# Unread products in the waits of a start-up, and another order of its first five chunks

## The chip, the cores and the metric

One core of a Trainium2 chip runs the program; the others are idle. The metric is the time of one execution on the device, in microseconds, as the median of several runs. Engines are named as in the profile: PE multiplies matrices (PEld is its weight load), DVE, ACT and POOL work element by element, SP issues most of the transfers (DMA). Each engine takes its own instructions in the order in which the program wrote them.

## The reference

Three stages follow each other. A recurrence per head with a 40x40 state, over 768 steps of 4x8 heads:

```
y[t]  = r[t] . state
Sa    = state . a[t]
state = state * w[t] - Sa (x) b[t] + v[t] (x) k[t]
```

Its output, 3072 tokens of 320 numbers, goes through a dense layer pair, `max(0.01 h, h)` of `h = x @ w_in` (320x2048), then `@ w_out` (2048x320), and then through a layer of eight experts, of which each token takes the one with the largest gate (320x1024, relu, 1024x320, times the gate's probability).

## The kernel before

The recurrence is cut into 24 chunks of 32 steps, all 32 heads together. A chunk `c` has a part that needs no state, and one that does.

The part without state (`prep`, lines 199 to 283): load `in`, the decays and `a` (`load1`), and `KB`, the keys and `b` (`load1b`); clamp and check the decays (steps a), scan them on DVE (b), scale the queries on POOL and take reciprocals (c), scan backwards on DVE (d), scale the keys on POOL and DVE (e), keep the queries in DRAM (f). Then four products with their evictions by DVE and ACT (G, H, I, J are the products on line 259, g, h, i, j the evictions on lines 264 and 265, into `Ms` and `KBr`), and z, which writes the small triangular matrices `Ms` to `Pq` by four transfers (line 277) and copies `Ms` and `KBr` to DRAM (line 280). Chunk 0 works in `KB`, `AtI`, `Ms`, `KBr`; chunks 1 and 2 keep the same things in pieces of the tiles `woh` and `wol`, which are free as yet; from chunk 3 on it is chunk 0's tiles again.

From `Pq` of several chunks a table T of inverses is made (`halves`): one transpose on DVE into `Tinv` (line 332), 28 small products and sums (lines 342 and 348), one transpose into `TT` (line 356). For chunks 0 and 1 (the word A in the order) this runs on DVE, for chunks 2 and 3 (B) on POOL.

The part with state: `l2`, `l3` load what the chunk needs; `s1` multiplies the state into the chunk (line 388), `s2` makes three products, with T, with `NT`, with T again (line 403), each after an eviction of the one before; `s3` makes the next state (428), `s3x`, `s4`, `s5` make the output (446, 458, 475), `s6` turns the state round (493). Then `s1` of the next chunk.

The dense layers work on pairs of chunks in half steps, the word H: eight products for 128 of the 2048 columns (`layer1`, line 705, into the banks psH), activation on ACT, DVE and POOL, six products of the second layer (line 721). Their weights come in 102 pieces of 256 columns, the word +: a load issued by ACT (line 610), a guard on ACT, three operations on DVE (lines 575, 577, 579), a cast on ACT and a difference on DVE (line 639 or 647).

What comes in which order is written out by hand: the string `START` for chunks 0 to 4, then `STEP`, `LATE`, `END` for one chunk each. `play` reads the words one after another and writes the instructions of each; p is one step of a later chunk's `prep`, u and v are one step of an inverse. So the order of words is the order on every engine. `START` ends in the profile near 218 us. The word F calls `keep_warm`, and no string before the change holds it.

Of the kernel before, what the change touches and what calls it, by code (L numbers as in the profile page):

```python
# [11 lines left out]
F32 = mybir.dt.float32  # L12
# [10 lines left out]
C = 32  # L23
# [13 lines left out]
LOAD, SPLIT = 18, 27  # L37

START = (
# [9 lines left out]
)  # L49
STEP = (  # L50
    "w s6a.-1 s1 s6b.-1 H H H s2 H H p w p p s3a H l2.1 H p w p w p w p w p s3b p s3x H H s4a p p s4b H p H w s5a s5b H p H p H w H w p H l3.1 "
# [449 lines left out]
class Moe1:  # L501


    def __init__(s, tc, ctx, i, k, xT, x2d, tbl, psH):
        s.tc = tc
        nc = s.nc = tc.nc
        s.i, s.k, s.xT, s.x2d, s.tbl, s.psH = i, k, xT, x2d, tbl, psH
        s.bank = lambda: s.psH.tile([128, 512], F32, name="psH")
        s.wide = mybir.dt.size(i["hwi"].dtype) == 8
        pool = lambda x, n, b: x.enter_context(tc.tile_pool(name=n, bufs=b, side="right"))  # L510
        s.r1, s.r2 = pool(ctx, "mr1", 1), pool(ctx, "mr2", 2)
        inner = s.inner = ctx.enter_context(ExitStack())
        s.psX = inner.enter_context(tc.tile_pool(name="psX", bufs=1, space=PSUM, side="right"))
        c = s.p1 = pool(inner, "mp1", 1)
        s.p2, s.p3 = pool(inner, "mp2", 2), pool(inner, "mp3", 3)
        s.wih = c.tile([128, 2, FF], F32R, name="wih")
        s.wil = c.tile([128, 2, FF], F32R, name="wil")
        s.wis = c.tile([128, FF], F32R, name="wis")

        s.tri = s.r1.tile([128, 128], BF16, name="tri")  # L520
        nc.gpsimd.memset(s.tri, 1.0)
        nc.gpsimd.affine_select(out=s.tri, in_=s.tri, compare_op=ALU.is_ge, fill=0.0, base=-1, pattern=[[1, 128]], channel_multiplier=-1)
        s.ones = s.r1.tile([128, 128], BF16, name="ones")
        nc.gpsimd.memset(s.ones, 1.0)
        s.raws = s.r1.tile([128, 4, 2 * DM], I32, name="raws")
        s.wg = s.raws.bitcast(F32).rearrange("p a (b d) -> p (a b) d", b=2)
        s.junk = s.r1.tile([128, DM], BF16, name="junk")
        s.run = s.r1.tile([128, E], BF16, name="run")
        s.code = s.r1.tile([128, E], F32, name="code")
        nc.gpsimd.iota(s.code, pattern=[[-1, E]], base=E, channel_multiplier=0, allow_small_or_imprecise_dtypes=True)  # L530
        s.ecap = s.r1.tile([128, E], F32, name="ecap")
        nc.gpsimd.iota(s.ecap, pattern=[[CAP, E]], base=0, channel_multiplier=0, allow_small_or_imprecise_dtypes=True)
        s.ids = s.r1.tile([128, NC], I32, name="ids")
        for b in range(B):
            for t in range(2):
                nc.gpsimd.iota(s.ids[32 * b:32 * b + 32, t::2], pattern=[[2 * C, NC // 2]], base=S * b + (C - BIG) * t, channel_multiplier=1)
        s.x2c = x2d.rearrange("(b c t) d -> c b t d", b=B, t=C)
        s.least = s.r1.tile([128, 1], F32, name="least")
        nc.gpsimd.memset(s.least, 2.0 ** -30)
        s.fill = s.r1.tile([128, 32], I32, name="fill")  # L540
        nc.gpsimd.memset(s.fill, BIG)
        s.none = s.r1.tile([128, 32], I32, name="none")
        nc.gpsimd.memset(s.none, 0)

    def lend(s):

# [146 lines left out]
    def layer1(s, f):  # L693
# [1 line left out]
        if f == 0:  # L695
            s.xh, s.xl = s.next
        o = slice(128 * f, 128 * f + 128)
        ps = s.psH.tile([128, 512], F32, name="psH")
        terms = [
            (s.wih[:, 0, o], s.xh[:, 0]), (s.wih[:, 1, o], s.xh[:, 1]), (s.wis[:, o], s.xh[:, 2]),  # L700
            (s.wih[:, 0, o], s.xl[:, 0]), (s.wih[:, 1, o], s.xl[:, 1]), (s.wil[:, 0, o], s.xh[:, 0]), (s.wil[:, 1, o], s.xh[:, 1]),
# [116 lines left out]
def stepwise(tc, ctx, i, k, x2d, tbl, plan):  # L818

    nc = tc.nc  # L820
    psH = ctx.enter_context(tc.tile_pool(name="fbH", bufs=2, space=PSUM, side="right"))
    m1 = Moe1(tc, ctx, i, k, None, x2d, tbl, psH)
    for _ in m1.weights():
        pass
# [368 lines left out]
def build(tc, i, out, dbg=None):  # L1193
    nc = tc.nc
    with ExitStack() as top:
# [8 lines left out]
        bad = cst.tile([128, NC + 20 + NF * DM // 256], F32, name="bad")  # L1204
        badi = cst.tile([128, 1], I32, name="badi")
        with ExitStack() as left, ExitStack() as ctx, ExitStack() as right:
            psH = ctx.enter_context(tc.tile_pool(name="psH", bufs=2, space=PSUM, side="right"))
            m1 = Moe1(tc, ctx, i, k, xT, x2d, tbl, psH)
            with ExitStack() as ctx2:
                psA = ctx2.enter_context(tc.tile_pool(name="psA", bufs=4, space=PSUM))  # L1210
                at = Attn(tc, ctx2, i, k, xT, bad, psA)
                own, m1.bank = m1.bank, at.bank
                half, routing = overlap(tc, at, m1, plan)
                m1.bank = own
            m2 = Moe2(tc, left, right, i, k, x2d, tbl, out, plan)

            bs = cst.tile([128, 1], F32, name="bs")
            nc.vector.tensor_reduce(out=bs, in_=bad, axis=AX.X, op=ALU.add)

            def check():  # L1220
                ps = m1.bank()
                nc.tensor.matmul(ps[0:1, 0:1], bs, k.one, start=True, stop=True)
                nc.vector.tensor_single_scalar(badi[0:1], ps[0:1, 0:1], 0.0, op=ALU.is_gt)

            tail(m2, half, check)
            m1.inner.close()
            m2.banks(m1.bank)
            m2.more()
            m2.go(routing, plan.make(m1))
        with tc.If(nc.values_load(badi[0:1, 0:1], min_val=0, max_val=1) > 0), ExitStack() as ctx:  # L1230
            stepwise(tc, ctx, i, k, x2d, tbl, plan)
        with ExitStack() as ctx:
# [2 lines left out]
            lo = nc.values_load(plan.lim[0:1, 0:1], min_val=0, max_val=NFIX - NE)  # L1235
            hi = nc.values_load(plan.lim[0:1, 1:2], min_val=0, max_val=NSLOT)
            m2.other(lo, hi)


def keep_warm(at, m1):  # L1240

    ps = at.bank()
    for _ in range(2):
        at.nc.tensor.matmul(ps.rearrange("q (a b) -> q a b", a=4), m1.ones, m1.ones[:, None, :].to_broadcast([128, 4, 128]), start=True, stop=True)


def overlap(tc, at, m1, plan):
# [69 lines left out]
    def play(order, here=0):  # L1317
# [4 lines left out]
        for word in order:  # L1322
# [36 lines left out]
            elif what == "C":  # L1359
                m1.clear()  # L1360
            elif what == "F":
                keep_warm(at, m1)
            elif what in "Ee":
                more(what == "E")
            elif what in "gd":
# [54 lines left out]
```

## Time and profile before

| | |
|---|---|
| median of 3 runs | 1122.68 us (1119.37 to 1127.97) |
| the profiled execution | 1121.85 us, its span 1120.1 us |
| PE busy | 953.4 us, 85% |
| DVE busy | 820.3 us, 73% |
| ACT, POOL busy | 527.8 us, 503.2 us |
| mean granted clock of PE | 0.946 |

The profiled execution lasts 1.75 us longer than its span, which runs from the first to the last instruction. Times in rows are from the span's start. In the 40 slices of the page PE is busy for 3 to 8 tenths in the first eight (224 us) and for 8 or 9 tenths in most of the others; DVE is busy for 7 to 9 tenths in the first ten.

### The profile page before, as it was taken

Reading aid. Unit: us, or ns where it says so; the run is one execution under the profiler, and the core shown is the slowest. Engines: PE = TensorE matmul, PEld = TensorE weight load, DVE = VectorE, ACT = ScalarE, POOL = GpSimd, SP = SyncE. Lnnn points to the kernel's source line nnn. Section 1 sums busy time; section 2 is a strip of 40 time slices with the busy share of each in tenths; the row PEclk is TensorE's granted clock in tenths of the full one; section 3 lists DMA queues with packets and bytes.
Section 4 is the critical chain, followed back from the end, with each engine's and each line's share of the span. In section 5 each row is a group of like instructions: output and inputs, shape, how many; then the busy total and the mean of one; then the engine's idle time right before and its main releaser. Section 6 shows DMA issues by size and latency. Waiting matters only on the chain. (4 is left out here: it accounts for less than half of the span.)

```text
span 1120.1 us, 40696 instructions
## 1 busy us (share of the span) xinstructions
PE 953.4 (85%) x16817; PEld 897.7 (80%) x16817; DVE 820.3 (73%) x1946; ACT 527.8 (47%) x1308; POOL 503.2 (45%) x690
## 2 busy tenths in 40 slices
PE   3476778978799899999899999999787799999993
PEld 3366676868788888888788888999777799999992
DVE  8989787757778777868786777676569677777760
ACT  4455454653344344444444344444444466666640
POOL 5123144215863498338843783334537123233220
PEclk9999986878999999999999999999898899999997
DMA  7878776855546654565645342334235653741620
GB/s 248 238 220 224 215 197 175 226 149 153 147 133 165 145 160 138 162 157 162 151 135 144 91 90 76 102 89 134 54 83 160 138 168 113 231 117 58 190 78 11
DMA packets 132379, 163.18 MB, mean 146 GB/s; under 512 B 67708, under 2 KB 89868, under 8 KB 132056
## 3 DMA queue, kind: packets, MB, share of 16 engines
q1 hardware_dynamic: 122071, 141.30, 46.7%
q10 hardware_dynamic: 5760, 10.49, 3.2%
q0 software_dynamic: 4352, 8.69, 2.6%
q8 instruction: 135, 2.21, 0.9%
q14 instruction: 61, 0.49, 0.2%
HBM read 127.61 MB, written 42.27 MB: 152 GB/s over the span
## 5 line engine op out<-in xcount | busy, mean ns | idle before, releaser
L712 POOL TENSOR_TENSOR gl<-g,gh 128x256 fp32r<-128x256 f32 x192 | 155.2, 811 | 224.5 <-ACT gh L711 194.2
L710 DVE TENSOR_TENSOR g<-psH,g 128x256 f32<-128x256 f32 x192 | 81.1, 423 | 117.1 <-ACT g L709 110.5
L711 ACT CAST gh<-g 128x256 fp32r<-128x256 f32 x192 | 77.9, 406 | 165.7 <-DVE g L710 158.1
L721 PE MATMUL psX<-woh,gl 128*128 128x320 f32 x384 | 125.1, 326 | 12.4 <-POOL gl L712 11.9
L721 PE MATMUL psX<-woh,gh 128*128 128x320 f32 x384 | 133.6, 348 | 1.2 <-ACT woh L638 1.1
L709 ACT ACTIVATE g<-psH 128x256 f32<-128x256 f32 x192 | 73.7, 384 | 119.5 <-PE psH L705 89.0
L721 PE MATMUL psX<-wol,gh 128*128 128x320 f32 x384 | 123.2, 321 | 0.2 <-issue 0.2
L742 DVE SCALAR_TENSOR_TENSOR junk<-X,raws 128x320 bf16<-128x320 f32 x192 | 113.6, 591 | 11.5 <-ACT X L739 9.0
L259 PE MATMUL psA<-AtI,KB 40*64 40x72 f32 x1408 | 72.1, 266 | 37.9 <-DVE KB L238 18.7
L259 PEld LDWEIGHTS psA<-AtI,KB 40*64 40x64 f32 x1408 | 63.9, 169 | 44.4 <-POOL woh L237 18.6
L1123 POOL DMA_INDIRECT out<-ey,sid x32 | 34.5, 1078 | 122.9 <-ACT ey L1122 63.2
L705 PE MATMUL psH<-xh,wih 128*128 128x256 f32 x384 | 86.8, 309 | 3.3 <-DVE g L710 2.9
L721 PEld LDWEIGHTS psX<-woh,gl 128*128 128x128 f32 x384 | 76.4, 199 | 15.8 <-POOL gl L712 15.7
L721 PEld LDWEIGHTS psX<-woh,gh 128*128 128x128 f32 x384 | 76.3, 199 | 7.3 <-ACT gh L711 1.5
L299 POOL TENSOR_TENSOR itmp<-Tinv 128x30 f32<-128x30 f32 (+14 forms) x120 | 69.9, 582 | 26.3 <-DVE Tinv L291 19.1
L705 PE MATMUL psH<-xl,wih 128*128 128x256 f32 x384 | 81.0, 294 | 0.3 <-DVE xl L690 0.3
L705 PE MATMUL psH<-xh,wil 128*128 128x256 f32 x384 | 80.5, 293 | 0.0
L721 PEld LDWEIGHTS psX<-wol,gh 128*128 128x128 f32 x384 | 76.6, 200 | 0.7 <-issue 0.4
L305 POOL TENSOR_TENSOR Tinv<-Tinv,itmp 128x30 f32<-128x30 f32 (+14 forms) x120 | 73.4, 611 | 7.8
L705 PEld LDWEIGHTS psH<-xh,wih 128*128 128x128 f32 x384 | 66.3, 200 | 8.3 <-DVE g L710 5.6
L705 PEld LDWEIGHTS psH<-xl,wih 128*128 128x128 f32 x384 | 63.3, 202 | 0.6 <-DVE xl L690 0.6
L1101 DVE SCALAR_TENSOR_TENSOR ehl<-psH,ehh 128x256 fp32r<-128x256 f32 x86 | 36.1, 420 | 37.7 <-ACT ehh L1100 34.9
(278 smaller groups left out, 2762.7 us busy)
## 6 DMA issues: line engine op xcount, KB each, us to landing
raw<-hwe SPq DMA_DIRECT2D x48, 512.0 KB
raw<-hwe SPq DMA_DIRECT2D x32, 640.0 KB
in<-h SPq DMA_DIRECT2D x23, 521.0 KB
KB<-h SPq DMA_DIRECT2D x22, 512.0 KB
L<-dKBr SPq DMA_DIRECT2D x24, 320.0 KB
dKBr<-KBr SPq DMA_DIRECT2D x22, 320.0 KB
lamY<-dl SPq DMA_DIRECT2D x24, 264.0 KB
dl<-lam SPq DMA_DIRECT2D x22, 264.0 KB
```

The costliest lines, as they stand in the source:

```text
L259: nc.tensor.matmul(v[64 * i:64 * i + 64, k, :], z["KB"][64 * i:64 * i + 40, p, :], z["AtI"][64 * i:64 * i + 40, p, :], start=True, stop=True)
L299: eng.tensor_tensor(out=box["v"], in0=T[:, k + 1:32, k:k + 1].to_broadcast([128, n, k]), in1=T[:, k:k + 1, 0:k].to_broadcast([128, n, k]), ...
L305: eng.tensor_tensor(out=T[:, k + 1:32, 0:k], in0=T[:, k + 1:32, 0:k], in1=box["v"], op=ALU.add)
L705: nc.tensor.matmul(ps[:, 0:256], w, x, start=(n == 0), stop=(n == 7))
L709: nc.scalar.activation(out=g, in_=ps[:, 0:256], func=AF.Copy, scale=0.01)
L710: nc.vector.tensor_tensor(out=g, in0=ps[:, 0:256], in1=g, op=ALU.max)
L711: nc.scalar.copy(out=gh, in_=g)
L712: return gh, gl, lambda: nc.gpsimd.tensor_tensor(out=gl, in0=g, in1=gh, op=ALU.subtract)
L721: nc.tensor.matmul(s.x2[t][:, 0:DM], x[:, o], w[:, f, :], start=(f == 0 and n == 0), stop=(f == NF - 1 and n == 2))
L742: nc.vector.scalar_tensor_tensor(out=s.junk, in0=X[:, t, 0:DM], scalar=1.0, in1=s.wg[:, e], op0=ALU.mult, op1=ALU.mult, accum_out=lg[:, t, ...
L1101: nc.vector.scalar_tensor_tensor(out=hl, in0=ps, scalar=0.0, in1=hh, op0=ALU.max, op1=ALU.subtract)
L1123: nc.gpsimd.indirect_dma_start(out=s.out, out_offset=bass.IndirectOffsetOnAxis(ap=ids[:, t:t + 1], axis=0), in_=y[:, t, :], in_offset=None ...
```

## The change

`START` gets 59 words F, all ahead of the first chunk's `s2.0`, and its other words in another order; each of them stands there as often as before. F no longer borrows a bank of the recurrence: it multiplies a 128x128 tile of ones (bf16) with itself six times, into columns 384 to 511 of the first of the two banks psH, and nobody reads that. The two banks were a pool that handed them out in turn; now they are two tiles with names, which `turn` hands out in turn as 384 columns.

```diff
 START = (
-    "E 0a 0b 0c 0d 1a 1b + + 1c 1d L.2 + + 0e 0f 0G + 0H 1e 1G 2a 0I 2b 1g l3.0 0g 1H 2c 2d 1I 0h L.3 + 1h 0i 1i 0J + 2e 1J 1j 0j + 0z 3a 2G 2g 2H + 2h 1z "
...
+    "0a 0b E F 0c 1a F F F F F 0d F F 1b F F 1c + + 1d L.2 F C 1f + + + F 0e F F F F F F F F 0f 1e F F F 2a F F F 0G 2b 2c 0g 1G 1g 2d 1H 1I 1J 0H 1h 1i "
+    "L.3 1j 0I 0h 0J + 0i + 2e 1z 0j 2G + F F 0z A K.3 F F 3a + 3b 3c 2g + 2H F 2I l3.0 3d F u + F 2h F F u + F 2i u F l2.0 + F F u u u u F u F 3e u F F F "
...
-        s.i, s.k, s.xT, s.x2d, s.tbl, s.psH = i, k, xT, x2d, tbl, psH
-        s.bank = lambda: s.psH.tile([128, 512], F32, name="psH")
+        s.i, s.k, s.xT, s.x2d, s.tbl = i, k, xT, x2d, tbl
+        s.two = [psH.tile([128, 512], F32, name=f"psH{n}") for n in range(2)]
+        s.turns = 0
+        s.bank = s.turn
...
+    def turn(s):
+
+        s.turns += 1
+        return s.two[s.turns % 2][:, 0:384]
+
+    def keep_warm(s):
+
+        for _ in range(6):
+            s.nc.tensor.matmul(s.two[0][:, 384:512], s.ones, s.ones, start=True, stop=True)
...
-        ps = s.psH.tile([128, 512], F32, name="psH")
+        ps = s.turn()
...
-def keep_warm(at, m1):
-
-    ps = at.bank()
-    for _ in range(2):
-        at.nc.tensor.matmul(ps.rearrange("q (a b) -> q a b", a=4), m1.ones, m1.ones[:, None, :].to_broadcast([128, 4, 128]), start=True, stop=True)
```

On PE, at the first products of the recurrence (line 259, now 260; `woh` is chunk 1, `wol` chunk 2, `AtI,KB` chunks 0 and 3), it was before:

```order
L259 MATMUL psA<-AtI,KB 64x72 x16
L259 MATMUL psA<-woh 64x72 x8
L259 MATMUL psA<-AtI,KB 64x72 x8
L259 MATMUL psA<-woh 64x72 x16
L259 MATMUL psA<-AtI,KB 64x72 x8
L259 MATMUL psA<-woh 64x72 x8
L259 MATMUL psA<-wol 64x72 x32
```

and is now:

```order
L556 LDWEIGHTS ones
L556 MATMUL psH_109<-ones 128x128
L260 MATMUL psA<-AtI,KB 64x72 x8
L260 MATMUL psA<-woh 64x72 x32
L260 MATMUL psA<-AtI,KB 64x72 x24
L260 MATMUL psA<-wol 64x72 x8
L556 LDWEIGHTS ones
```

The pair of the first two rows stands there 156 times ahead of the first product, and 198 times more between the product with `wol` and the first product with T. Chunk 1's four groups have moved ahead of chunk 0's last three.

On SP, at the transfers that bring the triangular matrices of chunks 0 and 1 to `Pq`, it was before:

```order
L277 DMA Pq<-Ms 32x256 x4
L280 DMA dMs<-Ms 128x512
L280 DMA dKBr<-KBr 128x640
L277 DMA Pq<-woh 32x256 x4
L280 DMA dMs<-woh 128x512
L280 DMA dKBr<-woh 128x640
L230 DMA dl<-lam 128x528
L196 DMA KB<-h 128x1024
```

and is now:

```order
L278 DMA Pq<-woh 32x256 x4
L281 DMA dMs<-woh 128x512
L281 DMA dKBr<-woh 128x640
L278 DMA Pq<-Ms 32x256 x4
L281 DMA dMs<-Ms 128x512
L281 DMA dKBr<-KBr 128x640
L197 DMA KB<-h 128x1024
L231 DMA dl<-lam 128x528
```

and on DVE, from the last eviction of chunk 0 to the transpose that reads `Pq`, it is now:

```order
L265 TENSOR_TENSOR Ms<-psA,mask 128x128
L590 SCALAR_TENSOR_TENSOR wt_t<-raws,wt_t 128x256
L652 TENSOR_TENSOR wil<-wt_x,wih 128x256
L213 TENSOR_SCALAR in_497<-in_497 128x16x32
L592 SCALAR_TENSOR_TENSOR wt_x<-raws,wt_t 128x256
L220 COPY d1r<-wol 128x16
L222 SCALAR_TENSOR_TENSOR lam<-in_497,d1r 128x528
L228 RECIPROCAL d1r<-lam 128x15
L265 TENSOR_TENSOR wol<-psA,mask 128x128
L588 TENSOR_SCALAR wt_t<-raws 128x256
L235 SCALAR_TENSOR_TENSOR il<-in_497,d1r 128x528
L333 STREAM_TRANSPOSE Tinv<-Pq 128x1024
```

(one reciprocal of a single column stands there too, after the row of the other). Chunk 1 now goes to `Pq` first, chunk 0 last, and the backward scan of chunk 3 stands ahead of the transpose, behind which it stood.

On SP, at the loads of `l3.1` (`Rr`, `Vt`), it was before:

```order
L484 DMA xT_77<-Y 40x4x128 x2
L242 DMA dA<-AtI 2048x1x32
L498 DMA L_178<-Z_1261 40x320 x2
L372 DMA Rr<-hr 40x1024
L373 DMA Vt<-hvt 40x1024
```

and is now:

```order
L499 DMA L_180<-Z_1442 40x320 x2
L231 DMA dl<-lam 128x528
L191 DMA in_1494<-h 128x1042
L243 DMA dA<-AtI 2048x1x32
L485 DMA xT_77<-Y 40x4x128 x2
L373 DMA Rr<-hr 40x1024
L374 DMA Vt<-hvt 40x1024
```

The queries' copy and the state's transfer have moved from behind the output's transfer to ahead of it.

## Rows read from the trace of the kernel before

**Rows 1.** Stretches: PE, PEld, DVE, ACT, POOL busy us (instructions), clock, DMA, GB/s.

```profile
18.70:28.00 9.30, 8.78 (x142) 8.57 (x144) 8.30 (x21) 3.96 (x14) 2.35 (x2) 1.00 0.61 181
28.00:35.30 7.30, 3.28 (x56) 3.06 (x52) 6.21 (x16) 5.16 (x15) 1.64 (x2) 1.00 0.60 201
35.30:52.70 17.40, 5.60 (x128) 5.08 (x129) 16.41 (x48) 7.62 (x23) 1.90 (x2) 1.00 1.03 246
52.70:218.30 165.60, 129.13 (x3206) 114.97 (x3206) 134.33 (x287) 86.04 (x236) 52.50 (x88) 0.90 0.76 210
```

**Rows 2.** Groups on PE from 0 to 150 us: count, busy us, mean ns.

```profile
L259 PE MATMUL psA<-AtI,KB 40*64 40x72 f32 x400 | 27.6, 322 | 36.7 <-DVE KB L238 18.7 <-POOL KB L237 13.1 <-issue 2.9
```

**Rows 3.** The same from 300 to 600 us.

```profile
L259 PE MATMUL psA<-AtI,KB 40*64 40x72 f32 x640 | 25.0, 229 | 0.0
```

**Rows 4.** PE in order of time, dense layer: start, us, operation, count.

```profile
147.39 0.63 PE L705 MATMUL psH<-xl,wih 128*128 128x256 f32 x2
147.82 0.63 PE L705 MATMUL psH<-xh,wil 128*128 128x256 f32 x2
...
160.24 0.40 PE L705 MATMUL psH<-xl,wih 128*128 128x256 f32 x2
160.47 0.40 PE L705 MATMUL psH<-xh,wil 128*128 128x256 f32 x2
```

**Rows 5.** Stretches around the first changes of the granted clock.

```profile
149.00:152.40 3.40, 2.31 (x56) 2.06 (x56) 3.33 (x7) 1.94 (x6) 1.04 (x4) 1.00 0.86 176
152.40:159.20 6.80, 6.48 (x66) 6.26 (x66) 6.46 (x16) 6.08 (x19) 4.15 (x10) 0.50 0.36 106
```

**Rows 6.** PE in order of time, the recurrence [idle before, released by].

```profile
18.66 2.19 PE L259 MATMUL psA<-AtI,KB 40*64 40x72 f32 x32 [18.66 <-DVE KB L238]
...
42.53 4.31 PE L259 MATMUL psA<-AtI,KB 40*64 40x72 f32 x64 [11.26 <-POOL KB L237]
...
52.71 1.29 PE L403 MATMUL psA<-RH,TT 32*32 32x40 f32 x64 [4.20 <-DVE TT L356]
...
60.91 1.11 PE L446 MATMUL psA<-ident,Xq 128*128 128x128 f32 x4 [2.48 <-ACT Xq L416]
...
94.08 1.08 PE L458 MATMUL psA<-Rr,Vt 40*32 40x32 f32 x64 [3.43 <-DMA Vt<-hvt]
...
187.38 0.79 PE L403 MATMUL psA<-RH,TT 32*32 32x40 f32 x64
```

**Rows 7.** POOL in order of time: the tile of ones.

```profile
4.67 0.55 POOL L524 MEMSET ones<- 128x128 bf16 x1
```

**Rows 8.** DVE in order of time, chunks 0 to 3 and the first inverse.

```profile
10.07 1.32 DVE L212 TENSOR_SCALAR L<-L 128x512 f32<-128x512 f32 x1 [0.56 <-ACT wchk L211]
...
27.70 0.28 DVE L264 TENSOR_TENSOR Ms<-psA,mask 128x128 f32<-128x128 f32 x1
...
35.32 1.93 DVE L332 STREAM_TRANSPOSE Tinv<-Pq 128x1024 f32<-128x1024 f32 x1 [0.65 <-DMA Pq<-woh]
37.16 1.23 DVE L234 TENSOR_TENSOR_SCAN il<-in,d1r 128x528 f32<-128x528 f32 x1
...
38.38 0.43 DVE L577 SCALAR_TENSOR_TENSOR wt_t<-raws,wt_t 128x256 int32<-128x256 int32 x1
...
40.76 0.69 DVE L238 SCALAR_TENSOR_TENSOR KB<-KB,il 128x512 f32<-128x512 f32 x1 [0.25 <-DMA KB<-h]
...
50.63 1.94 DVE L356 STREAM_TRANSPOSE TT<-Tinv 128x1024 f32<-128x1024 f32 x1
```

**Rows 9.** SP's issues in order of time: start, us in the queue.

```profile
24.41 5.38 SPq L277 DMA_DIRECT2D Pq<-Ms  x4
...
30.94 2.41 SPq L277 DMA_DIRECT2D Pq<-woh  x4
...
85.31 1.01 SPq L484 DMA_DIRECT2D xT<-Y  x2
...
88.89 0.44 SPq L372 DMA_DIRECT2D Rr<-hr  x1
```

More of the change, by code (lines that the diff above doesn't have):

```diff
@@ L820, in stepwise @@
     nc = tc.nc
-    psH = ctx.enter_context(tc.tile_pool(name="fbH", bufs=2, space=PSUM, side="right"))
+    psH = ctx.enter_context(tc.tile_pool(name="fbH", bufs=1, space=PSUM, side="right"))
     m1 = Moe1(tc, ctx, i, k, None, x2d, tbl, psH)
@@ L1206, in build @@
         with ExitStack() as left, ExitStack() as ctx, ExitStack() as right:
-            psH = ctx.enter_context(tc.tile_pool(name="psH", bufs=2, space=PSUM, side="right"))
+            psH = ctx.enter_context(tc.tile_pool(name="psH", bufs=1, space=PSUM, side="right"))
             m1 = Moe1(tc, ctx, i, k, xT, x2d, tbl, psH)
@@ L1361, in play @@
             elif what == "F":
-                keep_warm(at, m1)
+                m1.keep_warm()
             elif what in "Ee":
```

16 rows, old and new, of the table START are left out of this document.

## The prediction

> **What bounds the kernel now.** I first read the busy table by stretches, for who is busy in the part that the change touches. From 18.7 to 35.3 us PE works 8.78 + 3.28 = 12.06 us of 16.6 and DVE 14.5; from 35.3 to 52.7 us PE works 5.60 of 17.4 and DVE 16.41 [rows 1]. So up to the first product with T the bound is DVE's ordered list, and PE waits for it: 18.66 us ahead of the first product, 11.26 us ahead of chunk 3's, 4.20 us ahead of the first product with T [rows 6]. From 52.7 to 218.3 us, the rest of `START`, neither is full: PE is idle for 36.5 us and DVE for 31.3 us [rows 1]; a chain of steps that hop between engines sets the pace there. What follows is not changed, and later work keeps its order, so I let a microsecond won or lost in `START` arrive whole at the end.
>
> Then the clock. The table shows 1.00 up to 149 us, but nothing had been recorded by then, and the durations say something else. The products of line 259 take 322 ns on average up to 150 us and 229 ns later [rows 2, 3]. In the dense layer two products of 256 columns start 0.43 us after two others at 147 us and 0.23 us at 160 us [rows 4]: 0.215 us and 0.117 us each, 1.2 GHz and 2.4 GHz. So PE runs at 1.2 GHz through all of the part with F, and F can change that. How long it would last is to be seen behind the first rise: from 149.0 to 152.4 us PE, at 2.4 GHz, did nearly only the small products of the recurrence and worked 2.31 of 3.40 us; then the grant fell to 0.50 [rows 5]. The recurrence's own products do not hold the clock, so I expect 2.4 GHz while F runs and 1.2 GHz again soon after `s2.0`.
>
> **What an F costs.** No row has a bf16 product of 128 columns. By columns it is half of a dense product: 0.108 us at 1.2 GHz, 0.059 us at 2.4 GHz [rows 4]. From above, the four 128x128 transposes took 1.11 us, 0.28 us each [rows 6]. I take the columns' price, since there too each product has its own weight load, and nothing shows that the transposes of f32 are like it. 59 words make 354 products. 156 stand ahead of the first real product and start when the ones are there, at 5.2 us [rows 7]; they have 13.4 us until 18.66 us and need 9.2 us at 2.4 GHz, 16.8 us at 1.2 GHz. 198 stand between the products of chunks 2 and 3 and `s2.0`. From 18.66 to 52.71 us PE has 34.05 us, of which 12.06 + 5.60 = 17.7 us are used [rows 1, 6]; 16.4 us are free, 0.083 us for each. At 2.4 GHz they need 11.7 us and are hidden by DVE's list; at 1.2 GHz 21.4 us, and are not. With the clock rising inside the first block I cost all F at nothing; the other end is 3.4 + 5.0 = 8.4 us late.
>
> [...]
>
> **The inverse comes sooner.** Chunk 0's last eviction was at 27.70 us, the transpose that reads `Pq` at 35.32 us [rows 8]. Between them SP issued chunk 0's four writes, two copies, and chunk 1's four writes up to 33.35 us [rows 9]; the data came 1.97 us later. Now chunk 1's writes and copies go out while chunk 0's last three groups are evicted, and behind the last eviction there are only four writes, 2.41 + 1.97 = 4.4 us: `Pq` is there at 32.4 us if the last eviction stays. It does: the same DVE instructions stand ahead of it in another order. DVE itself has 11 instructions between the eviction and the transpose where it had 16 in 6.21 us busy [rows 1]; with two scans of 1.2 us and nine of 0.1 to 0.4 us [rows 8] I get 5.0 us, the transpose at 33.0 us, 2.3 us sooner. From there to the end of the second transpose it took 17.25 us [rows 8]. Now one scan of 1.23 us is gone from that stretch, and four more operations on weights (0.43 us each) and one more eviction (0.28 us) [rows 8] are in it: 0.75 us more. So T is ready 1.6 us sooner: **-1.6 us** (0 to -3.2). DVE waits for chunk 3's keys there (0.25 us) [rows 8]; their load is issued behind the same `z` as before, so it moves with the rest.
>
> **The loads of weights start later.** ACT issued the first four at the start and now behind the check of chunk 0; SP's first loads have the transfers to themselves. ACT's issues then stand ahead of chunk 1's check, for which DVE waited 0.56 us [rows 8], and chunk 0's backward scan (1.2 us), which had filled that gap before, is now behind it. I take **+0.6 us** (-0.5 to +1.2).
>
> **Three products with T.** They took 1.29 us each at 1.2 GHz and 0.79 us at 2.4 GHz [rows 6], on the path, since DVE and ACT wait for each. 42 products of F stand just ahead. Three times 0.5 us is 1.5 us at most; I take **-1.0 us** (0 to -1.5).
>
> **Behind `s2.0`** the words between two products with T are nearly the same in kind and number, so I give the reordering nothing, with one exception. PE waited 3.43 us for `Vt` at 90.65 us [rows 6]: `l3.1` stood on SP behind the output's transfer, a copy and the state's transfer, and was issued at 88.89 us, 2.57 us after the output's transfer [rows 9]. The copy and the state's transfer are now ahead. 2.57 us of the wait goes, but what is late next is DVE's masking, so I take **-1.5 us** (0 to -2.6).
>
> The two named banks alternate as the pool did, and F's columns are no one else's: nothing. The cleared tables' two transfers move to SP's start, where SP waits for scans: nothing, and about 1 us (two issues near 0.44 us [rows 9]) if that cover is gone.
>
> **Sum.** -1.6 + 0.6 - 1.0 - 1.5 = -3.5 us on the profiled execution's 1121.85 us, 1118.4 us. That execution lies 0.8 us below the median of the runs, so the median comes out at **1119 us**. A difference under 1%, 11.2 us, can hardly be told here: the three runs of before lie 8.6 us apart.
>
> **Rivals.**
> A. PE sets the pace after all, and half of its busy time at 1.2 GHz from 18.7 us to the end of `s2.0` comes back: 12.06 + 5.60 + three products of 1.29 = 21.5 us, half is 10.8 us, 1112 us. For it speaks that every step of the chain has a PE part. Against it, DVE was busy 16.41 of the last 17.4 us [rows 1]. Chance 0.12. [...]
> B. The new order removes waits from 52.7 to 218.3 us. If 40% of DVE's idle 31.3 us goes, 12.5 us, together with the rest of the sum 16 us: 1107 us. For it, the idle time is there, and 3.43 us of it is one named wait; against it, the words between the products with T are the same. Chance 0.15.
> C. F's products block PE. 354 of them have 13.4 + 16.4 = 29.8 us; at 0.108 us they delay by 8.4 us (1131 us), from 0.116 us on by more than 1%, and at the transposes' 0.28 us by 69 us (1192 us). The evictions of chunks 2 and 3 wait on PE's queue behind them, DVE's list behind those. It decides if a weight load and its product do not overlap or the clock stays at 1.2 GHz. Against it, dense products with their own weights start at the columns' pace [rows 4]. Chance 0.15, of which 0.09 above 1%.
> D. T comes sooner, but the operations on weights that were pushed behind it hold the later steps, and all is as before: 1123 us. Chance 0.13.
> The forecast has 0.45.
>
> **The numbers.** Faster by over 1%: B and half of A, 0.21. Slower by over 1%: 0.09 of C and 0.02 for an unforeseen wait, 0.11. Within 1%: 0.68. The range reaches down to B and up to C at 1.2 GHz, 1107 to 1131 us, and leaves out the rest of C and half of B, under 2 in 10.
>
> **What the next profile would show.** The granted clock rises near 10 us and falls near 55 to 60 us; line 259 takes near 230 ns ahead of that; the transpose into `Tinv` starts near 33 us, the first product with T near 51 us without PE being the one that is late; PE's wait for `Vt` at chunk 1 is under 2 us. I am wrong if the first product with T starts after 52.7 us with F just ahead of it, or if the stretch from there to the end of `START` changes by more than 5 us, which the argument gives no reason for.

## The result, and the profile after

The change makes the kernel slower by 1.0%: 1136.37 us, median of 10 runs (1131.1 to 1140.88), against 1123.36 us, median of 10 runs of the kernel before on the same chip. The ratio is 1.0099, with a 95% interval of 1.0072 to 1.0127. The forecast was 1119 us, the range ended at 1131 us. The profiled execution took 1137.1 us, with a span of 1135.4 us, 15.3 us more than before's.

First the busy table by stretches of the changed kernel: three stretches up to the first product with T, which answer to [rows 1], then from each first product with T to the next chunk's, for chunks 0, 1 and 2 to 4. Columns as there.

```profile
18.70:28.00 9.30, 7.63 (x138) 7.18 (x140) 8.75 (x22) 4.43 (x15) 2.35 (x2) 0.64 0.78 187
28.00:34.20 6.20, 6.20 (x93) 5.60 (x90) 5.20 (x10) 4.60 (x11) 1.64 (x2) 0.71 0.82 280
34.20:55.00 20.80, 17.19 (x300) 15.87 (x300) 17.63 (x55) 8.11 (x23) 1.48 (x2) 0.75 0.89 217
54.96:80.08 25.12, 16.86 (x566) 15.08 (x564) 21.55 (x42) 13.77 (x38) 11.33 (x23) 0.58 0.70 198
80.08:120.96 40.88, 25.00 (x691) 22.16 (x685) 29.57 (x67) 17.54 (x49) 7.25 (x12) 0.50 0.78 206
120.96:196.60 75.64, 61.64 (x1362) 54.68 (x1365) 60.29 (x126) 38.89 (x108) 26.53 (x43) 0.60 0.69 194
```

The same three last stretches of the kernel before:

```profile
52.71:75.40 22.69, 16.86 (x556) 15.13 (x556) 19.50 (x43) 11.52 (x32) 5.12 (x12) 1.00 0.79 209
75.40:111.82 36.42, 25.38 (x695) 22.74 (x694) 31.88 (x67) 19.22 (x55) 13.43 (x24) 1.00 0.84 236
111.80:187.40 75.60, 61.08 (x1362) 54.30 (x1362) 59.25 (x124) 39.24 (x107) 25.85 (x43) 0.84 0.71 199
```

The stretches grow by 2.4, 4.5 and 0.0 us. PE's busy time in them does not, and F has no instruction there: what grew is waiting. Not all of it has to be the change: e5_banks below, with the instructions of before, takes 23.3 and 37.9 us for the first two. Where before waited for DVE ahead of the first product with T [rows 6], F now fills PE: 17.19 us of the 20.80.

PE of the changed kernel in order of time, with F on line 556, as far as it answers to [rows 6]:

```profile
5.28 11.63 PE L556 MATMUL psH<-ones 128*128 128x128 bf16 x156 [5.28 <-POOL ones L527]
...
49.58 2.10 PE L556 MATMUL psH<-ones 128*128 128x128 bf16 x18
51.61 0.97 PE L389 MATMUL psA<-Vx,At 32*32 32x40 f32 x64
52.51 2.52 PE L556 MATMUL psH<-ones 128*128 128x128 bf16 x42
54.96 0.72 PE L404 MATMUL psA<-RH,TT 32*32 32x40 f32 x57
...
98.53 1.25 PE L459 MATMUL psA<-Rr,Vt 40*32 40x32 f32 x62 [2.07 <-ACT Vt L449]
...
112.57 3.31 PE L260 MATMUL psA<-AtI,KB 40*64 40x72 f32 x48 [5.58 <-POOL KB L238]
...
120.96 1.29 PE L404 MATMUL psA<-RH,TT 32*32 32x40 f32 x64 [1.74 <-ACT wchk L214]
```

DVE in order of time, which answers to [rows 8]:

```profile
34.16 1.93 DVE L333 STREAM_TRANSPOSE Tinv<-Pq 128x1024 f32<-128x1024 f32 x1
...
47.78 0.29 DVE L265 TENSOR_TENSOR Ms<-psA,mask 128x128 f32<-128x128 f32 x1 [1.06 <-PE psA L260]
...
49.69 0.29 DVE L265 TENSOR_TENSOR Ms<-psA,mask 128x128 f32<-128x128 f32 x1 [1.28 <-PE psA L260]
...
52.35 1.99 DVE L357 STREAM_TRANSPOSE TT<-Tinv 128x1024 f32<-128x1024 f32 x1
...
110.80 0.69 DVE L239 SCALAR_TENSOR_TENSOR KB<-KB,il 128x512 f32<-128x512 f32 x1 [5.15 <-DMA KB<-h]
```

SP's issues, which answer to [rows 9], and ACT's between them:

```profile
92.15 0.43 SPq L366 DMA_DIRECT2D At<-dMs  x1
92.63 0.36 SPq L367 DMA_DIRECT2D At<-dA  x1
93.03 0.33 SPq L368 DMA_DIRECT2D Vx<-hv  x1
94.81 0.66 SPq L369 DMA_DIRECT2D L<-dKBr  x1
96.05 0.64 SPq L278 DMA_DIRECT2D Pq<-Ms  x1
96.95 0.52 SPq L278 DMA_DIRECT2D Pq<-Ms  x1
99.29 0.34 ACTq L623 DMA_DIRECT2D raws<-hwi  x1
100.72 0.51 SPq L278 DMA_DIRECT2D Pq<-Ms  x1
103.56 0.51 SPq L278 DMA_DIRECT2D Pq<-Ms  x1
105.67 0.33 SPq L197 DMA_DIRECT2D KB<-h  x1
```

Three things are to be seen. In this execution the inverse starts 1.2 us sooner than before (34.16 against 35.32 us) but ends later, since DVE waits twice for chunk 3's products, which stand behind 18 and 6 products of F. Behind the first product with T the late thing is another: `KB` of chunk 6. Its load is issued at 105.67 us, behind four writes of `Pq` that take SP from 96.05 to 104.07 us; POOL waits 10.63 us for it, DVE 5.15, and PE 5.58 us for POOL. In the kernel before, the same four writes took 2.91 us from 91.03 us on, the load was issued at 95.15 us, POOL waited 6.79 us for it and DVE 1.23. POOL of the changed kernel, then SP and POOL of the kernel before:

```profile
110.91 1.61 POOL L238 TENSOR_TENSOR KB<-KB,il 128x512 f32<-128x512 f32 x1 [10.63 <-DMA KB<-h]
```

```profile
91.03 2.91 SPq L277 DMA_DIRECT2D Pq<-Ms  x4
95.15 0.43 SPq L196 DMA_DIRECT2D KB<-h  x1
101.75 1.68 POOL L237 TENSOR_TENSOR KB<-KB,il 128x512 f32<-128x512 f32 x1 [6.79 <-DMA KB<-h]
```

And chunk 2's four loads, `l2.2`, stand ahead of the four writes now; before they were behind KB's load, at 99.50 us.

How four loads hold four writes is to be seen in SP's waits. Ahead of the four writes of `Pq` SP waited 0.5 us for `Vt<-hvt`, 0.2 us for `lamY<-dl`, 3.2 us for `At<-dA` and 2.3 us for a load of weights, `raws<-hwi`; the last two waits stand ahead of the third and the fourth write. `At<-dA` is one of the four loads of `l2.2`, issued 8.1 us ahead of the third write. The load of weights was issued by ACT at 99.29 us, 4.3 us ahead of the fourth. The four rows have 0.51 to 0.64 us each, the waits are in the gaps. In the kernel before, SP waited 0.7 us for `dA<-AtI` and 0.4 us for `raws<-hwi` ahead of the same four writes. Why a write waits for a transfer with which it has no tile in common, no view shows.

### The profile page after: what moved, and what is told of

It is laid out like the page before. It is cut to its first block, busy times and chain, and to the rows that moved or that the text cites. A ratio compares the mean times of both kernels' runs of the same rounds, so it can differ in the third digit from the quotient of the medians.

```text
span 1135.4 us, 41417 instructions
## 1 busy us (share of the span) xinstructions
PE 985.2 (87%) x17171; PEld 926.2 (82%) x17171; DVE 822.5 (72%) x1946; ACT 527.4 (46%) x1308; POOL 501.5 (44%) x690
## 5 line engine op out<-in xcount | busy, mean ns | idle before, releaser
L476 PE MATMUL psA<-Rr,L 104*40 104x32 f32 (+1 forms) x1536 | 47.8, 217 | 20.5 <-DVE Rr L462 11.3
```

Of the source, the lines that this page charges most:

```text
L476: nc.tensor.matmul(ps[64 * i:64 * i + 40, 32 * p:32 * p + 32], L[0:r, place(n), :], s.Rr[0:r, n, :], start=True, stop=True)
```

## The experiments

Where chunk times are given, they are counted in the trace: line 388 has 64 products for each chunk, line 403 192 for chunks 0 to 3. "Chunk 8" is the first product of its `s1`, 331.0 us in before and 341.2 us in the change.

| kernel | ratio to before (95%) | chunk 2's first product with T | chunk 8 |
|---|---|---|---|
| the change, first time | 1.0099 (1.0072 to 1.0127) | 121.0 | 341.2 |
| the change, e11_again | 1.0124 (1.0084 to 1.0164) | 118.0 | 342.1 |
| e1_no_f | 1.0143 (1.0114 to 1.0172) | 118.5 | 339.8 |
| e2_f_alone | 1.0070 (1.0035 to 1.0106) | 116.2 | 330.3 |
| e3_head | 1.0017 (0.9988 to 1.0046) | 112.3 | 330.6 |
| e4_tail | 1.0135 (1.0099 to 1.0172) | 119.6 | 339.7 |
| e5_banks | 0.9996 (0.9956 to 1.0036) | 113.8 | 330.0 |
| e6_l22_back | 1.0062 (1.0027 to 1.0096) | 114.0 | 342.7 |
| e7_l22_fwd | 1.0008 (0.9973 to 1.0043) | 118.7 | 330.6 |
| e8_warm_tail | 1.0081 (1.0042 to 1.0120) | 124.8 | 339.8 |
| e9_late | 1.0059 (1.0024 to 1.0094) | 112.5 | 332.6 |
| e10_early | 1.0079 (1.0048 to 1.0109) | 120.2 | 335.0 |
| e12_after_kb | 1.0120 (1.0085 to 1.0156) | 111.9 | 330.8 |
| e13_before_kb | 1.0054 (1.0028 to 1.0080) | 112.4 | 327.7 |
| e16_before_kb11 | 0.9956 (0.9922 to 0.9990) | 112.7 | 327.4 |
| e17_after_kb11 | 1.0029 (1.0001 to 1.0058) | 112.4 | 337.6 |
| e18_head_kb11 | 0.9964 (0.9939 to 0.9990) | 112.6 | 328.8 |

The ratios rest on 6 to 12 executions each, the two times on one profiled execution, and that one varies. e3_head profiled again (e15_head_again) reaches chunk 8 at 324.9 us, not 330.6. The instructions of e12_after_kb and e17_after_kb11 are the same on SP up to 244 us, and they reach it at 330.8 and 337.6. e5_banks, with before's instructions, has chunk 2's product 2.0 us later than before (111.8 us). So a difference of a few us at chunk 8, up to about 7, says nothing by itself here; what an edit costs is read from the ratio.

**Is it F or the order?** Four kernels, all with the two named banks. e1_no_f is the change with all F gone:

```diff
-    "0a 0b E F 0c 1a F F F F F 0d F F 1b F F 1c + + 1d L.2 F C 1f ...
+    "0a 0b E 0c 1a 0d 1b 1c + + 1d L.2 C 1f ...
```

> The changed order with all 59 words F left out; the two named banks stay. Theory Q (the F products, standing in PE's queue ahead of chunk 3's products and the first product with T, cost the time): everything comes back, the first product with T starts near 51 us as forecast, and the time is 1120 to 1124 us. Theory O (the new order of the words, above all on SP, costs about 7 us between the first and the third product with T): the first product with T starts near 51 to 52 us, but the stretch from it to chunk 2's is still about 7 us longer than before's 59.1 us, and the time is 1127 to 1130 us. Theory L (708 more instructions in PE's program shift where PE waits for nothing recorded, 2.75 us at 680 us in the profile of the change): the stretch from chunk 19's to chunk 21's steps, 5.4 us longer in the change, is as before here.

e2_f_alone is before's order with the 59 F put in:

```diff
-    "E 0a 0b 0c 0d 1a 1b + + 1c 1d L.2 + + 0e 0f 0G ...
+    "E 0a 0b 0c F 0d F F 1a F F ...  (26 ahead of 0G; 4 ahead of 2H, 1 of 2I, 14 of 3G, 3 of 3I, 1 of 3J, 3 of s1.0, 7 of s2.0)
```

> The order of before with 59 words F put in: 26 ahead of chunk 0's first product, 33 between the same products as in the change (4 and 1 ahead of chunk 2's second and third, 14 ahead of chunk 3's first, 3, 1, 3 and 7 behind that up to the first product with T). Theory Q: nearly all of the change's loss is here, the first product with T starts 2 us or more later than before's 52.7 us, and the time is 1130 to 1136 us. Theory O: the first product with T starts at 53 to 56 us, the stretch from there to chunk 2's is 59 us as before, and the time is 1124 to 1127 us. Theory L: about 5 us more on top, between 640 and 700 us, 1129 to 1132 us.

e3_head and e4_tail cut both orders at `s2.0`, where the same words lie behind both but for `2f` and `C`:

```diff
+e3_head: the change's words up to s2.0, without F; then before's, without C, with 2f behind s3a.0
+e4_tail: before's words up to s2.0; then the change's, without 2f, with C behind s5a.0
```

> No F. The changed order up to the first product with T, and behind it the order of before (chunk 2's last check scan stands a few words behind it, as in the change). Theory Q and theory O both: the first product with T starts near 51 us, the steps behind it keep before's distances, 1120 to 1123 us. A third theory, that the head of the new order leaves work undone that the tail then pays for (the pieces of the first inverse or of the weights): the second product with T is 2 us or more later than before relative to the first, 1125 to 1130 us.

> No F. The order of before up to the first product with T, and behind it the changed order. Theory O: chunk 2's product with T starts 5 to 8 us later than before's 111.8 us, POOL and DVE wait there for the load of KB that SP issues behind the four writes of Pq, and the time is 1128 to 1131 us. Theory Q: all as before, 1122 to 1125 us.

Without F the loss is all there (1.0143), so F is not what costs in the changed order; theory Q is out. The tail alone makes it (1.0135), the head alone does not (1.0017). Theory O has the place, but not the size: it expected at most 1130 and 1131 us, and 1138.01 and 1136.66 were measured. The head does what was forecast: its first product with T starts at 51.6 us, 1.1 us sooner than before's, and 0.6 us sooner in its second profile. What becomes of that gain can't be told: chunk 8 comes 0.4 us sooner than before's in the one and 6.1 us in the other, and the ratio's interval reaches from -1.3 to +5.2 us. F alone in before's order costs 0.7%, between the theories' forecasts; its first product with T is 2.2 us late, yet chunk 8 is where it was in before, so its profile shows no loss of START; it was long from chunk 8 to 22 (401.9 us). Some 3 us of this are found in the last experiment; why F costs more than that in this order stays open.

**The change once more.** e11_again is the changed kernel itself.

> The changed kernel itself once more, with a profile of another execution. Its stretch from chunk 8 to chunk 22 took 400.1 us where before's took 395.0, with the same instructions. Theory P (the program's other length or START's other end leave a lasting effect): 399 to 403 us again. Theory N (it varies by that much from run to run): anything from 392 to 403 us, and what remains of the loss lies in START, 8 to 12 us.

Its PE in order of time:

```profile
45.94 1.18 PE L556 MATMUL psH<-ones 128*128 128x128 bf16 x18
47.04 0.79 PE L389 MATMUL psA<-Vx,At 32*32 32x40 f32 x64
47.77 2.52 PE L556 MATMUL psH<-ones 128*128 128x128 bf16 x42
51.81 0.71 PE L404 MATMUL psA<-RH,TT 32*32 32x40 f32 x57 [1.52 <-DVE TT L357]
```

Here the same 18 products of F take 1.18 us, not 2.10, and PE waits for T, as forecast, 3.15 us sooner than in the first profile. The execution took 1140.57 us all the same, 3.5 us more than the first: chunk 2's product is still 3.0 us sooner, chunk 8 0.9 us later. In this pair the sooner T did not reach the end. The stretch from chunk 8 to chunk 22 took 401.4 us, as the first time (400.1).

**The banks.**

```diff
-        s.bank = lambda: s.psH.tile([128, 512], F32, name="psH")
+        s.two = [psH.tile([128, 512], F32, name=f"psH{n}") for n in range(2)]
+        s.bank = s.turn
```

> The order of before, no F, only the two named banks. Every engine's instructions up to about 750 us are the same as before's. Theory N (the banks cost nothing, as the prediction said): 1120 to 1125 us. Theory B (the banks cost the 5 to 8 us by which the stretch from chunk 8 to chunk 22 was longer than before's 395.0 us in the change and in the four kernels that had them): that stretch takes 400 to 403 us here too and the time is 1126 to 1129 us. If the stretch takes 400 us and the time is that of before, before's profiled 395 us was the low end of what this stretch takes from run to run.

Nothing that shows, as forecast: 0.9996; chunk 8 to 22 took 395.7 us.

**The four loads.** e6_l22_back and e7_l22_fwd move the one word, in the change and in before:

```diff
-s5b.0 + u l3.1 u l2.2 + + p ... + s4b.1 + p
+s5b.0 + u l3.1 u + + p ... + s4b.1 l2.2 + p
```

```diff
-p l3.1 u p + u ... s4b.1 + p l2.2 + s5b.1
+p l3.1 l2.2 u p + u ... s4b.1 + p + s5b.1
```

Theory S, against which theory W is set in both, says that the four loads hold the four writes of `Pq`, and with them the load of KB behind them. For e6_l22_back it gave KB's load near 97 us in place of 105.7, 36.5 us in place of 40.9 from chunk 1's first product with T to chunk 2's, and a time of 1131 to 1133 us.

> The change, with one word moved back: chunk 2's four loads (l2.2) stand behind the fourth step of chunk 1 again, not right behind chunk 1's l3. [...] Theory W (the late eviction of chunk 5's last group, 4 us behind before's, does it, since chunk 1's masking and product now stand ahead of the pieces of chunk 5): the distance stays at 40 to 41 us and the time at 1135 to 1138 us.

> The order of before with the pool's banks and one word moved: chunk 2's four loads (l2.2) right behind chunk 1's l3, as in the change. Theory S: the four writes of Pq take 6 to 8 us on SP instead of 2.9, KB's load is issued 4 to 5 us later than at 95.15 us, the first product with T of chunk 2 starts at 115 to 117 us instead of 111.8, and the time is 1126 to 1129 us. Theory W: at most 1 us is lost there and the time is 1122 to 1125 us.

SP, POOL and PE of e6_l22_back in order of time, each engine by itself:

```profile
92.63 4.06 SPq L278 DMA_DIRECT2D Pq<-Ms  x4
97.90 0.40 SPq L197 DMA_DIRECT2D KB<-h  x1
103.37 1.18 POOL L238 TENSOR_TENSOR KB<-KB,il 128x512 f32<-128x512 f32 x1 [4.31 <-DMA KB<-h]
113.99 1.29 PE L404 MATMUL psA<-RH,TT 32*32 32x40 f32 x64 [1.49 <-DVE TT L357]
```

The same of e7_l22_fwd:

```profile
96.00 6.19 SPq L277 DMA_DIRECT2D Pq<-Ms  x4
104.02 0.40 SPq L196 DMA_DIRECT2D KB<-h  x1
108.64 1.68 POOL L237 TENSOR_TENSOR KB<-KB,il 128x512 f32<-128x512 f32 x1 [13.38 <-DMA KB<-h]
118.73 1.29 PE L403 MATMUL psA<-RH,TT 32*32 32x40 f32 x64 [0.58 <-DVE TT L356]
```

The place is settled, both ways round: moved forward, the four loads alone make KB's load 8.9 us late and chunk 2's product 6.9 us; moved back, KB's load comes 7.8 us sooner and the distance between the two products with T shrinks from 40.9 to 34.4 us. Theory S holds there. Its price does not: in before's order the 6.9 us are gone by chunk 8, and the ratio is 1.0008; its interval ends at 4.8 us, so they do not arrive whole. In the changed order moving them back is worth about half of the loss, by the middles of intervals that overlap; its profile is no sooner at chunk 8 (342.7 us) than the change's two (341.2 and 342.1), so where that half was won is not shown. Before's order behind the four loads makes their delay good. That it makes good whatever comes late is not so, as the next experiment shows.

**The two halves.** At chunk 3's first product with T both orders have the same words behind them. e9_late and e10_early are cut there, without F:

```diff
+e9_late: before's words up to s2.3, then the change's
+e10_early: the change's words up to s2.3, then before's
```

> No F. The order of before up to the first product with T of chunk 3, and the changed order behind it: at that word both orders have the same words behind them. Theory E (the loss is made early, by KB's load that SP issues late between the products with T of chunks 1 and 2): as before up to there, and 1121 to 1125 us. Theory R (the new order of the dense layer's units and the inverse's pieces behind it loses as much or takes away the slack in which before's order makes good what is late): 4 us or more are lost between that product and chunk 8's first step, 190.7 us apart in before, and the time is 1126 to 1132 us.

> No F. The changed order up to the first product with T of chunk 3, and the order of before behind it. Theory E: that product starts at 146 us as without F, 6 us late, this stays, and the time is 1128 to 1132 us. Theory R: before's order makes good most of the delay up to chunk 8's first step, as in the kernel with only the four loads moved, where 6.9 us at chunk 2 were gone at chunk 8, and the time is 1122 to 1126 us.

Both cost: 0.59% and 0.79%, together 1.38%, the whole order 1.43%. So theories E and R are each about half of it, by the middles of the intervals. The early half costs with before's late half behind it. Its profile has it 7.4 us late at the cut and 4.0 at chunk 8. The profiled execution of e9_late took 1124.1 us where the median was 1128.38, and is 1.6 us late at chunk 8; which of the moved words there cost is not settled.

**KB's load ahead of the writes.** This takes the wait away where it arises, in the function that plays the pieces of `prep`; at piece 14 `f()` issues the four writes and two copies:

```diff
+                if n == 14 and c < NC - 1:
+                    at.load1b(c + 1)
                 f()
...
-                if n == 14:
-                    if c < NC - 1:
-                        at.load1b(c + 1)
```

> The change (with F), and in the preparation of every chunk the load of the next chunk's KB is issued ahead of the four writes of Pq and the two copies, not behind them. Theory S (the late issue of KB's load on SP is what the early half of the new order costs): the load of chunk 6's KB is issued 6 to 9 us sooner than at 105.7 us, POOL's 10.6 us and DVE's 5.2 us of waiting for it are gone, the product with T of chunk 2 starts at 113 to 116 us instead of 121.0, and the time is 1127 to 1131 us. Rival D (the eviction of chunk 5's last group and DVE's list behind it set the pace there, KB's wait only shows it): that product starts after 119 us and the time stays at 1135 to 1138 us.

> The kernel before with the same edit: KB's load ahead of the writes of Pq, for every chunk. Theory S: POOL's wait of 6.79 us and DVE's of 1.23 us for KB at 101.7 us get shorter, chunk 2's product with T starts 1 to 3 us sooner than at 111.8 us; if START then keeps it, 1117 to 1120 us. Theory G (what is won or lost ahead of the dense layer's units is given back by chunk 8, as the 1.1 us of the sooner T and the 6.9 us of the moved loads were): 1120 to 1123 us.

In the changed order chunk 2's product comes at 111.9 us, 9.1 us sooner than in the change and sooner than theory S forecast. In before's it comes at 112.4 us, no sooner than before's 111.8, which theory S had wrong. Both reach chunk 8 early, at 330.8 and 327.7 us, by 10.4 and 3.3 us. Behind it they lost that and more: chunk 8 to 22 took 402.2 and 408.2 us, the ratios are 1.0120 and 1.0054, and theory S's forecasts of the time (at most 1131 and 1120 us) were passed by 6.6 and 11.6 us. So the last three make the edit for chunks 4 to 10 alone, `c < 11` in the first condition and `11 <= c < NC - 1` in the second.

> The kernel before, with KB's load ahead of the writes of Pq only for the chunks prepared in START (4 to 10), as before's for the rest. Theory M (the same edit for all chunks won 3.3 us up to chunk 8 and lost 13 us between chunks 8 and 22, where the writes of Pq were held up by the load): chunk 8's first step comes 2 to 5 us sooner than before's 331.0 us, the stretch from chunk 8 to 22 takes 392 to 400 us, and the time is 3 to 5 us below before's. Theory G (won time is given back): within 2 us of before.

> The change, with KB's load ahead of the writes of Pq only for the chunks prepared in START (4 to 10). Theory M: chunk 8's first step comes near 331 us as in the same edit for all chunks, without the loss behind it, and of the change's 13 us some 8 go: the ratio to before is 1.002 to 1.007, what the late half costs. If the ratio stays at 1.010 or more, KB's load was not what the early half loses.

> The changed order up to the first product with T, before's behind it, no F, and KB's load ahead of the writes of Pq for chunks 4 to 10. If the 0.6 to 1.1 us of the sooner T and what KB's load wins add up and stay: 4 to 6 us below before. If START's end does not keep them: within 2 us of before.

SP, POOL and PE of e17_after_kb11:

```profile
94.18 0.36 SPq L197 DMA_DIRECT2D KB<-h  x1
96.28 8.10 SPq L278 DMA_DIRECT2D Pq<-Ms  x4
101.34 1.96 POOL L238 TENSOR_TENSOR KB<-KB,il 128x512 f32<-128x512 f32 x1 [5.04 <-DVE Rr L462]
112.36 1.29 PE L404 MATMUL psA<-RH,TT 32*32 32x40 f32 x64 [1.63 <-DVE TT L357]
```

The writes still take 8.10 us, but KB's load is not behind them any more, and nobody waits for it. Of the change's 1.0% to 1.2% there are 0.29% left, inside theory M's range, though chunk 8 came at 337.6 us and not near 331. In the kernel before the same edit wins 0.44%, so about 0.4 of the 0.7 to 0.95 points are won in either order. The rest, 0.3 to 0.5 points, would be what the change had lost there, but the intervals of these ratios reach 0.3 points to either side, so it is not clear of the noise. Where the edit wins in before's order is not shown: chunk 2's product is no sooner there (112.7 us). e16_before_kb11 (1112.23 us beside 1117.25) is 0.4% faster than the kernel before, e18_head_kb11 (1114.49) as well; 2.8 us is less than the 4 to 6 forecast for the case that the sooner T adds to the edit, and no such addition shows.

**Would a high clock have been worth it?** e8_warm_tail as run has before's order with 41 words F between `s2.0` and the first H, one behind every fourth word, and none ahead; its expectation names another split.

```diff
-s2.0 B + p s3x.0 + u p + s3a.0 u p s4a.0 ...
+s2.0 B + p F s3x.0 + u p F + s3a.0 u p F s4a.0 ...
```

> The order of before with 26 words F ahead of chunk 0's first product, none up to the first product with T, and 15 from there to the first products of the dense layer, one behind every fourth... word of that stretch (90 products between 52.7 and 133 us). It asks whether a high clock up to 133 us would be worth anything. Theory H (every step of the chain has a product on its path, and at 2.4 GHz each takes half): if the granted clock is at 1.0 in more than half of 52 to 133 us, the first products of the dense layer come 4 to 8 us sooner than before's 133.1 us. Theory I (DVE's list sets the pace there): they come within 2 us of 133. If the clock stays at 0.5, the products only stand in the way and it is 0 to 3 us later.

```profile
75.69 1.46 PE L555 MATMUL psH<-ones 128*128 128x128 bf16 x12
```

The profile gives a mean grant of 0.65 from 75 to 125 us and 0.50 from 125 to 150 us, 12 products of F took 1.46 us, and the first products of the dense layer came at 148.2 us instead of 133.1. The expectation gave 0 to 3 us for products that only stand in the way; it was 15.1 us in the profile and 0.8% in the ratio. A clock held high there was not reached, so the question stays open.

**The stretch behind START.** From chunk 8 to 22 the instructions of before and of all kernels but e12 and e13 are the same. Two kernels that had been long there ran once more:

> The kernel of the changed order without F once more, for the profile of another execution. Theory P (what is lost behind chunk 8 belongs to the kernel): its stretch from chunk 8 to chunk 22 takes 399 to 403 us again (401.6 us there the first time, 395.0 us in before). Theory N (it varies from execution to execution): anything from 392 to 403 us.

> The kernel with only the head of the changed order once more, for the profile of another execution. Theory P: 399 to 403 us between chunk 8 and chunk 22 as the first time (400.7 us), and a time of 1125 to 1128 us. Theory N: anything from 392 to 403 us, and a time between 1119 and 1130 us that goes with it.

398.1 us after 401.6, and 395.9 after 400.7 (with 1116.46 us in all): theory N for a good part, in kernels without F. The change's 400.1 and 401.4 us beside before's 395.0 are another matter, since they sit in one place. From chunk 8 to chunk 19 both its profiles take 318.0 us and before's 317.6; from chunk 19 to chunk 21 they take 57.0 and 56.2 us and before's 52.6. In there PE stops in the middle of chunk 20's 64 products on line 476 and waits for nothing that the profile shows ("issue"), for 2.75 us in the first profile of the change and 3.26 us in the second. The first:

```profile
680.53 1.61 PE L476 MATMUL psA<-Rr,L 104*40 104x32 f32 x41 [2.75 <-issue]
```

This was theory L of e1_no_f and e2_f_alone. All six profiles with the 59 words F stop at these products, for 1.89 to 3.26 us, and take 55.1 to 57.0 us from chunk 19 to 21, e2_f_alone 55.6. None of the others stops there; of the thirteen without F eleven take 52.6 to 54.2 us, e1_no_f 52.7 as theory L had it, and e13_before_kb and e16_before_kb11 55.5 and 56.9. So the 59 words F go with some 3 us lost at a place 600 us behind the last of them. What PE waits for there was not found out.

## Why the prediction was wrong

**The step that failed** is "Behind `s2.0` the words between two products with T are nearly the same in kind and number, so I give the reordering nothing". The words were not that near in number: from chunk 0's first product with T to chunk 1's the change has 61 where before has 48, 20 of them steps u of the inverse in place of 9, and from there to chunk 2's 75 in place of 86. And the number does not decide: what counts on SP is which transfer stands ahead of which. In place of nothing, the tail alone gives 1.0135: the early half 0.8% (the head is in it), in which KB's load behind the four writes is the wait that was found, the late half 0.6% without a cause found. The rule "I am wrong if ... the stretch from there to the end of START changes by more than 5 us" caught it: 165.6 us became 171.9 (174.2 in the second profile). The other sign, the first product with T after 52.7 us with F just ahead of it, came in the first profile too (54.96 us) and not in the second (51.81). Rival B had the place and the wrong sign: the new order adds waits.

**"I let a microsecond won or lost in `START` arrive whole at the end"** failed too, for the 6.9 us lost by the four loads in before's order (1.0008). The 3.15 us between the two profiles of the change did not show in their totals. For the 1.1 us won by the head the runs are too coarse.

**The inverse sooner and the weights' loads** (-1.6 and +0.6 us, together -1.0) were right in place and size: -1.1 us in e3_head and -0.6 us in its second profile, with the transpose into `Tinv` at 33.94 us in the first, forecast 33.0.

**F at nothing** held in the changed order, where leaving F out brought nothing back (1.0143), and its price by columns held as well: 18 in 2.10 us at 0.50 and in 1.18 us at 1.00. In before's order F alone costs 0.7%, and some 3 us of that stand at chunk 20, where the prediction did not look. That F can change the clock was right: 22 of its products stand between 8 and 10 us and 39 between 12 and 14 us, and the products of line 260 that follow took 222 ns at the least, where those of line 259 before took 324. That the clock would stay high while F runs was not: 0.64 to 0.75 on average in the first three stretches. No run shows a clock in GHz. What the prediction calls 1.2 and 2.4 GHz are the two paces of [rows 4], 0.215 and 0.117 us for 256 columns, 1.19 and 2.19 columns per ns, and its sums use the paces. In the change two such products start 0.43 us after two others at 144 us, where the grant was 0.50. The first profile shows rival C at small size, 2.25 us late at the first product with T with F just ahead, the second does not, and its total is not the shorter one (1140.57 us against 1137.1). In e11_again 42 products of F in a row took 2.52 us at 1.00, 0.060 us each.

**The products with T at the high clock**: 0.72 and 0.79 us came true for two, at a grant of 1.00 from 54 to 58 us, the third took 1.20 us from 59.11 us on, at 0.50, and it did not matter. **`Vt`**: the wait of 3.43 us shrank to 2.07 us, for ACT's copy instead of the load, where the prediction had named DVE's masking; with the stretch around it 4.5 us longer, it did not help. **The banks**: nothing, and nothing showed.

## What to carry to other kernels

When words that issue transfers change places, look up what each transfer waits for, transfers issued on other queues included, and who stands behind it on the same queue: here two of four small writes waited 3.2 and 2.3 us for loads of other tiles, the four took 8 us in place of 3, and a load stood behind them. Before a delay ahead of a busy stage is counted, ask whether the stage gives it back; 6.9 us here were worth nothing in before's order. And one profile shows where a wait is, not what it costs: one and the same kernel reached chunk 8 at 330.6 and at 324.9 us.

## What was not expected of the hardware

One and the same program was granted different clocks in two executions. From 41.9 to 52.0 us PE was busy for all of 10.10 us in the first profile of the change, and the grant was 0.50; in the second profile the stretch that holds the same products of F and of the recurrence had 1.00.

```profile
41.90:52.00 10.10, 10.10 (x143) 9.08 (x143) 7.35 (x31) 3.32 (x10) 0.00 (x0) 0.50 0.88 196
```

```profile
37.40:51.80 14.40, 12.16 (x287) 11.26 (x286) 13.68 (x48) 7.50 (x23) 1.18 (x1) 1.00 0.92 236
```

Ahead of it PE had waited 3.61 us for DVE in the first. From 58.9 to 150 us, where no F stands, both had 0.50.
